# Moving eleven zero fills from GpSimd's queue to SyncE's and ScalarE's queues in a decode backward kernel

## The chip, the cores and the metric

The kernel runs on one core of a Trainium2 chip. The metric is device time in microseconds (us), the slowest core of one launch. Most executions agree within 0.3%. "Before" is the kernel without the change and "after" the kernel with it.

The engines are TensorE (PE in the profile), VectorE (DVE), ScalarE (ACT), GpSimd (POOL) and SyncE (SP). In the profile sixteen DMA engines move the data, and SyncE, ScalarE and GpSimd issue the transfers.

## The reference, cut to what matters

```python
# D 448, 16 query heads, 8 KV heads, Dh 256, caches of Sk = 32768 rows, window W = 4096, F 1792
def _fwd_reference(...):
    h  = x + attention(layernorm(x), k_cache[:, :, Sk - W:], v_cache[:, :, Sk - W:]) @ wo
    h2 = h + ((layernorm(h) @ w_gate) * (layernorm(h) @ w_up)) @ w_down
    return h2
# outputs: h2, and the gradients of h2 (against grad_out) with respect to
#          x, k_cache, v_cache, wq, wo, w_gate, w_up, w_down      -> out_0 .. out_8
```

Only the last 4,096 of 32,768 cache rows are attended to. So seven eighths of the two cache gradients (out_2 and out_3, 134 MB each) are zeros that have to be written. These zero fills are most of the kernel's bytes.

## The kernel before: the parts that matter

One large on-chip tile, the "arena", holds everything. Its first 8,192 columns (`zeros`) are the source of a 2 MB fill: 128 rows of 16 KB. The FFN later needs the second half of these columns for weights, so 13 fills of the middle read the first half twice ("half fills"). A memset gives the second half back to the fills after the FFN.

```python
HALF0, HALF1 = 42, 55
LD = nc.sync; ZQ = nc.gpsimd

def send_fills(n0, n1, halves=False):
    for reg in fills[n0:n1]:
        if halves: ZQ.dma_start(out=reg..., in_=zeros[:, 0:ZW // 2]...)   # first half, twice   (cut)
        else:      ZQ.dma_start(out=reg, in_=zeros)

send_fills(0, HALF0)                 # 42 full fills
send_fills(HALF0, HALF1, True)       # 13 half fills
...
# attention, head by head; K and V of the later heads are loaded into buffers that earlier heads free
after = {0: [("K", 3), ("V", 3)], 1: [("K", 4), ("V", 4), ("K", 5)], 2: [("V", 5)], 3: [("V", 6), ("K", 6)], 4: [("K", 7)], 5: [("V", 7)]}
for g in range(G):
    p_f = p_next
    if g + 1 < G: p_next = scores(g + 1)      # needs K of head g + 1
    moments(g, p_f)
    for kind, n in after.get(g, []): load_kv(...)          # on SyncE   (cut)
    if g == G - 2: load_wo(0)
load_wo(1)
load_block(0); load_block(1)                  # FFN weights: w_gate and w_down on SyncE, w_up on ScalarE
for n in range(3):                            # three blocks of the FFN
    ...                                       # reductions over the weights, last: dhn
    if n + 2 < 3: load_block(n + 2)
    if n == 1:
        nc.vector.memset(ar(ZW // 2, ZW // 2), 0.0)        # gives the fills their second half back
        send_fills(HALF1, len(fills))                      # 48 full fills
...
# backward of attention: 4 MB of cache gradients per head and the weight gradients, all stored by SyncE
for o, g, n0, n1, f in late_jobs:             # last 18 MB of zeros, issued by SyncE
    ...
```

## Time and profile before

| what | before | where it is read |
|---|---|---|
| time, median (lowest to highest) | 801.93 us (801.87 to 802.2) | three runs |
| span of the profiled execution | 800.5 us | first line of the page |
| bytes moved | 334.84 MB | page, part 2 |
| PE busy | 57% | page, part 1 |
| DMA engines busy | 9 tenths or more in 39 of 40 slices | page, part 2 |

These are lines of parts 2 and 3 of the page of before. Part 2 cuts the span into 40 slices of 20 us: the digit is the DMA engines' mean busy share in tenths, below it the rate. Part 3 gives packets, MB and share of time by queue: q0 is GpSimd's, q1 SyncE's, q10 ScalarE's.

```profile
DMA  9999999999999999999999999999999999999994
GB/s 350 431 430 429 428 430 430 427 428 428 431 426 422 428 417 409 420 422 428 433 423 425 424 430 428 429 426 426 424 427 423 426 420 425 423 424 427 423 440 192
q0 software_dynamic: 16496, 216.01, 63.8%
q1 hardware_dynamic: 11382, 116.68, 34.7%
q10 hardware_dynamic: 1440, 1.61, 0.6%
```

The DMA engines never rest before the last slice. So the kernel is bound by its transfers, and a change that moves no bytes away can only win in the last slice, unless packets take less time (a busy engine can also be a slow one, as skew_end_hi16k below shows). Here is that slice in steps of 2 us, from the windows view of before. After the five engines' busy times come the granted TensorE clock, the share of the 16 DMA engines that is busy, and GB/s.

```profile
786.00:788.00 2.00, 0.00 (x0) 0.00 (x0) 0.00 (x0) 0.00 (x0) 0.00 (x0) 0.50 0.79 336
788.00:790.00 2.00, 0.00 (x0) 0.00 (x0) 0.00 (x0) 0.00 (x0) 0.00 (x0) 0.50 0.54 229
790.00:792.00 2.00, 0.00 (x0) 0.00 (x0) 0.00 (x0) 0.00 (x0) 0.00 (x0) 0.50 0.27 115
...
794.00:796.00 2.00, 0.00 (x0) 0.00 (x0) 0.00 (x0) 0.00 (x0) 0.00 (x0) 0.50 0.12 49
...
798.00:800.00 2.00, 0.00 (x0) 0.00 (x0) 0.00 (x0) 0.00 (x0) 0.00 (x0) 0.50 0.02 8
```

No compute engine works any more. A share of 0.06 is one DMA engine of sixteen. The engines run dry one after the other from 786 us on, and the last one works alone to 799 us.

The records do not name the DMA engine of a packet. But packets of one engine follow each other almost without a gap (from 780 us on in before, 90% of the steps from one to the next are under 0.04 us), so they can be put into sixteen chains. Which chain is which engine stays unknown; where the chains end is clear. In before the last three end at 791.4, 795.3 and 799.0 us, and all sixteen at 790.1 us on the mean. The quantities "last end", "mean end" and "idle" below come from these chains, of one profiled execution each. The spans of nine executions of before in one batch ran from 799.9 to 801.0 us, so a difference under about 1 us between two last ends says little.

Two lines of the waits of before (engine, line, what it waited for: us in total, times, longest), six of its timeline (start, length, what; in brackets the idle time before it and what ended that; no bracket, no wait) and one of its windows will be needed again. In the timeline, 155.46 is where PE begins with the K cache of head 4:

```profile
PE ao_ps L376 <- DMA arena<-in_A_wo_dram: 10.7, 1, 10.7
PE tr_ps L252 <- DMA arena<-in_A_k_cache_dram: 8.4, 3, 3.9
```

```profile
155.46 1.07 PE L252 MATMUL tr_ps<-ident_bf,arena 128*128 128x128 bf16 x16
347.66 0.67 POOL L130 DMA_DIRECT2D out_dram<-arena  x1 [4.86 <-DMA out_dram<-arena]
366.85 0.17 DVE L406 COPY gu_f<-gu_ps 128x10 f32<-128x10 f32 x1 [12.66 <-PE gu_ps L405]
372.55 1.76 DVE L428 MEMSET arena<- 128x2048 uint32 x1 [0.41 <-DVE hh_f L409]
374.61 2.65 POOL L132 DMA_DIRECT2D out_dram<-arena  x5 [26.28 <-DVE arena L428]
484.57 56.83 SPq L648 DMA_DIRECT2D out_dram<-arena  x6
```

```profile
340.00:385.00 45.00, 14.10 (x104) 8.65 (x102) 24.39 (x54) 3.81 (x9) 4.52 (x8) 0.50 1.02 426
```

GpSimd issued its last half fill at 347.66 us, waited 26.28 us for the memset, and went on at 374.61. SyncE began to store gradients at 484.57 us.

### The profile page before, as it was taken

The numbers are of one execution on the slowest core, as the hardware profiler recorded it, in microseconds if no ns is written. First come the engines' busy times: TensorE is split into PE (matmuls) and PEld (weight loads), VectorE is DVE, ScalarE is ACT, GpSimd is POOL, SyncE is SP. The second block draws the span as 40 slices with busy tenths as digits, with TensorE's granted clock in tenths as the row PEclk, the third lists the DMA queues.
The fourth block names the chain that finished last, engine by engine and source line by source line (L and its number), as shares of the span: only waits on it lengthen the run. The fifth ranks groups of instructions, "written<-read, shape, count | busy, mean of one in ns | idle before, by whom it ended". The sixth has DMA issues, their size and how long they took to land.

```text
span 800.5 us, 8486 instructions
## 1 busy us (share of the span) xinstructions
PE 459.3 (57%) x3182; PEld 245.9 (31%) x3182; DVE 370.2 (46%) x1176; ACT 196.3 (25%) x309; POOL 62.0 (8%) x112
## 2 busy tenths in 40 slices
PE   0459999999999994623239295845262064520000
PEld 0334554545545552312129143322021022200000
DVE  2115363472552652255770975766681187660000
ACT  0143313224133100000002054643241045340000
POOL 4000000010100110101100010000000000000000
PEclk9978999999999997555559699776557567655555
DMA  9999999999999999999999999999999999999994
GB/s 350 431 430 429 428 430 430 427 428 428 431 426 422 428 417 409 420 422 428 433 423 425 424 430 428 429 426 426 424 427 423 426 420 425 423 424 427 423 440 192
DMA packets 29359, 334.84 MB, mean 418 GB/s; under 512 B 2819, under 2 KB 5894, under 8 KB 7814
## 3 DMA queue, kind: packets, MB, share of 16 engines
q0 software_dynamic: 16496, 216.01, 63.8%
q1 hardware_dynamic: 11382, 116.68, 34.7%
q10 hardware_dynamic: 1440, 1.61, 0.6%
q8 instruction: 25, 0.41, 0.2%
q14 instruction: 16, 0.13, 0.0%
HBM read 53.69 MB, written 280.59 MB: 418 GB/s over the span
## 4 chain that ended last, share of the span: by engine, by line
PE 35%; DMA 33%; DVE 15%; ACT 4%; issue 2%; another core or an unknown queue 0%; SPq 0%; ACTq 0%; DVEq 0%
DMA out_dram<-arena 19%; PE M_ps L311 11%; PE ok_ps L315 6%; PE rows_ps L255 6%; PE tr_ps L252 4%; DMA dh_bc<-in_grad_out_dram 4%; DMA arena<-in_A_k_cache_dram 4%; ACT arena L269 2%; DMA arena<-in_A_wo_dram 2%; DVE arena L645 2%; DVE arena L454 2%; DVE arena L646 2%; DMA arena<-in_B_w_up_dram 2%; PE dqb_ps L497 2%; DMA arena<-in_B_w_gate_dram 2%; DVE arena L509 2%
## 5 line engine op out<-in xcount | busy, mean ns | idle before, releaser
L307 DVE TENSOR_SCALAR arena<-arena,p_f 128x256 bf16<-128x256 bf16 x512 | 109.8, 280 | 67.0 <-PE M_ps L311 67.0
L311 PE MATMUL M_ps<-arena 128*128 128x512 bf16 x512 | 122.9, 381 | 0.0
L255 PE MATMUL rows_ps<-arena,vpad 128*16 128x512 bf16 x256 | 85.9, 431 | 22.2 <-DVE arena L608 16.9
L252 PE MATMUL tr_ps<-ident_bf,arena 128*128 128x128 bf16 x1024 | 87.9, 236 | 15.0 <-DMA arena<-in_A_k_cache_dram 8.4
L132 POOL DMA_DIRECT2D out_dram<-arena x90 | 48.8, 544 | 560.7 <-DMA out_dram<-arena 522.7
L252 PEld LDWEIGHTS <-arena 128*128 128x128 bf16 x1024 | 65.9, 105 | 65.0 <-issue 55.4
L638 PE MATMUL d_ps<-arena,rT 32*128 32x512 bf16 x256 | 43.6, 511 | 69.6 <-DVE arena L646 50.2
L269 ACT COPY arena<-tr_ps 128x1024 bf16<-128x1024 bf16 x64 | 61.7, 1015 | 87.9 <-PE tr_ps L252 87.9
L311 PEld LDWEIGHTS <-arena 128*128 128x128 bf16 x512 | 46.2, 99 | 50.8 <-issue 6.5
L315 PE MATMUL ok_ps<-arena 128*16 128x256 bf16 x512 | 57.5, 273 | 0.9 <-DVE arena L296 0.9
L606 ACT COPY arena<-tr_ps 128x1024 bf16<-128x1024 bf16 x32 | 32.5, 1016 | 96.1 <-PE tr_ps L252 39.3
L642 ACT CAST arena<-d_ps 128x512 bf16<-128x512 f32 x64 | 37.6, 588 | 71.5 <-PE d_ps L638 71.5
L645 DVE CAST arena<-d_ps 128x512 bf16<-128x512 f32 x64 | 43.9, 686 | 14.9 <-PE d_ps L638 14.6
L315 PEld LDWEIGHTS <-arena 128*16 128x16 bf16 x512 | 45.4, 90 | 13.9 <-issue 3.4
L646 DVE CAST arena<-d_ps 128x512 bf16<-128x512 f32 x64 | 43.5, 680 | 8.3 <-DMA out_dram<-arena 8.3
L638 PEld LDWEIGHTS <-rT 32*128 32x128 bf16 x256 | 11.2, 95 | 95.4 <-issue 52.1
L643 ACT CAST arena<-d_ps 128x512 bf16<-128x512 f32 x64 | 38.0, 594 | 9.1 <-DMA out_dram<-arena 9.1
L255 PEld LDWEIGHTS <-vpad 128*16 128x16 bf16 x256 | 18.9, 91 | 57.1 <-issue 49.3
L318 ACT COPY arena<-M_ps 128x512 f32<-128x512 f32 x16 | 8.6, 589 | 75.0 <-PE M_ps L311 75.0
L509 DVE CUSTOM_DVE_ANT_0 arena<-arena 128x4096 bf16<-128x4096 bf16 x3 | 13.1, 4422 | 23.1 <-ACT arena L502 23.1
L608 DVE COPY arena<-tr_ps 128x1024 bf16<-128x1024 bf16 x32 | 21.7, 680 | 4.1 <-PE tr_ps L252 4.0
L631 DVE TENSOR_SCALAR arena<-R_sb,tl_f 128x512 bf16<-128x512 bf16 x64 | 17.8, 347 | 2.1 <-ACT R_sb L628 1.9
(198 smaller groups left out, 358.1 us busy)
## 6 DMA issues: line engine op xcount, KB each, us to landing
out_dram<-arena POOLq DMA_DIRECT2D x103, 2048.0 KB, 53.5
out_dram<-arena SPq DMA_DIRECT2D x18, 2048.0 KB, 32.7
arena<-in_A_v_cache_dram SPq DMA_DIRECT2D x10, 2048.0 KB, 49.6
arena<-in_A_k_cache_dram SPq DMA_DIRECT2D x8, 2048.0 KB, 29.7
out_dram<-arena SPq DMA_DIRECT2D x4, 4096.0 KB, 57.2
arena<-in_A_wq_dram SPq DMA_DIRECT2D x2, 3072.0 KB, 20.5
arena<-in_A_wo_dram SPq DMA_DIRECT2D x2, 1792.0 KB, 16.2
out_dram<-arena SPq DMA_DIRECT2D x2, 1792.0 KB, 33.2
```

The source lines that it names most:

```text
L132: ZQ.dma_start(out=reg, in_=zeros)
L252: nc.tensor.transpose(tr_ps[:, dh, i, :], X_sb[:, 4 * q + i, dh * 128:(dh + 1) * 128], ident_bf[:])
L255: nc.tensor.matmul(rows_ps[:], lhsT=pad[:, dh, 16 * q:16 * q + 16], rhs=XT[:, dh].rearrange("p t k -> p (t k)"), start=(q == 0 and dh == 0 ...
L269: sT_ps = dots(kv_at(K_off[g]), KT_slot, vpad[g % 2], rows1, ps_c, "cols", lambda q, XT, ps: nc.scalar.copy(out=XT, in_=ps))
L307: nc.vector.tensor_scalar(out=pK[:, i, hh, :], in0=K_sb[:, t, :], scalar1=p_f[:, 8 * i + c, hh:hh + 1], scalar2=None, op0=ALU.mult)
L311: nc.tensor.matmul(M_ps[:, vh, :], lhsT=V_sb[:, t, vh * 128:(vh + 1) * 128], rhs=pK[:, i, :, :].rearrange("p h d -> p (h d)"), start=(t == ...
L315: nc.tensor.matmul(ok_ps[:, k, :], lhsT=ppad[g % 2][:, 8 * (t % 4) + t // 4, :], rhs=X_sb[:, t, :], start=(g == 0 and k == 0 and t == 0), ...
L638: nc.tensor.matmul(d_ps[:, qi].rearrange("p w d -> p (w d)"), lhsT=rT[32 * q:32 * (q + 1), :], rhs=RB_[32 * q:32 * (q + 1), l, :], start=T ...
L642: nc.scalar.copy(out=stV[:, t:t + 2, :], in_=d_ps[:, :, 0, :])
L643: nc.scalar.copy(out=stK[:, t:t + 2, :], in_=d_ps[:, :, 1, :])
L645: nc.vector.tensor_copy(out=stV[:, t:t + 2, :], in_=d_ps[:, :, 0, :])
L646: nc.vector.tensor_copy(out=stK[:, t:t + 2, :], in_=d_ps[:, :, 1, :])
```

## The change

Its intent: take work off GpSimd's queue. Of the fills, 92 stay there instead of 103. Six go on SyncE's queue behind K and V loads of the middle heads, two half fills on ScalarE's queue behind its last FFN load, three on SyncE's behind the last FFN load. The FFN loads are reordered: w_down first, the 64-row pieces ahead of the 384-row pieces, block 1 tied behind the second load of wo.

```diff
-HALF0, HALF1 = 42, 55
+HALF0, HALF1 = 36, 48
+SYNC = 11
 ...
+    own = fills[len(fills) - SYNC:]
+    fills = fills[:len(fills) - SYNC]
 ...
+    def fills_behind(eng, ins, n, halves=False):
+        with behind(ins):
+            for _ in range(n):
+                fill(eng, own.pop(), halves)
 ...
             for kind, n in after.get(g, []):
                 if kind == "K":
-                    load_kv(K_off[n], A_k_cache, n)
+                    ins = load_kv(K_off[n], A_k_cache, n)
 ...
+            if g in (2, 3, 4):
+                fills_behind(LD, ins, 2)
 ...
     def load_block(n):
+        last = [None, None]
+        LD.dma_start(out=wd, ...)                       # moved up from the end
         for eng, i, wt in ((LD, 0, B_w_gate), (nc.scalar, 1, B_w_up)):
-            eng.dma_start(out=wgu[:, 0:3, i, :], ...)
             eng.dma_start(out=wgu[0:DQ, 3, i, :], ...)
+            last[i] = eng.dma_start(out=wgu[:, 0:3, i, :], ...)
-        LD.dma_start(out=wd, ...)
+        return last
     load_block(0)
-    load_block(1)
+    with behind(wo_ins):
+        load_block(1)
 ...
-            if n + 2 < len(BLOCKS):
-                load_block(n + 2)
+            if n == 0:
+                last = load_block(2)
+                fills_behind(nc.scalar, last[1], 2, True)
             if n == 1:
                 nc.vector.memset(ar(ZW // 2, ZW // 2), 0.0)
                 send_fills(HALF1, len(fills))
+                fills_behind(LD, last[0], 3)
```

(The dots mark cuts.)

## The prediction

> **What bounds the kernel now.** Bytes: 334.84 MB in an 800.5 us span. In the windows view (20 us stretches) the mean share of the 16 DMA engines is 0.99 to 1.03 from 20 to 780 us. The chain of waits runs through PE (busy 57%), but the zero fills keep transfers going meanwhile. The only unfilled time is the start (0.92 in the first 20 us) and the end: in 2 us windows the share is about 1.0 until 786 us, then 0.79, 0.54, 0.27, 0.10, 0.12, 0.06, 0.02. One engine runs alone to 799 us, while an even share-out would end near 790. About 9 us (1.1%) is the most that reordering these bytes can win, unless packets also stall less.
>
> **What the change does.** Bytes and compute stay the same. GpSimd issues 92 fills, not 103; SyncE gets 6 behind the loads of heads 4 to 7 and 3 after the last FFN load, ScalarE 2. The Trainium skill ("DMA: Bandwidth & Descriptors", section "Issuing engines are not separate DMA queues") says the issuers share the 16 engines and interleave; the trace agrees: from 40 to 120 us GpSimd's queue moved 213 GB/s and SyncE's 214, together the full rate.
>
> 1. K of head 4 now queues behind two fills. Before, K3, V6, K4 landed at 124.1, 134.0, 144.0 us, 9.9 us apart. The build order puts two fills between K3 and V6, so K4 should land near 163.5. PE wants it at 155.5 and waits about 8 us. Later heads keep their 31.3 us cadence.
> 2. FFN: block 1's w_up load moves ahead of block 0's on ScalarE's queue, but waits there for all full-size fills (about 313 us). Block 0 is later by 5 to 10 us; block 1 and the memset that reopens the fills (before at 372.5 us) stay within 5 us.
> 3. Cover: GpSimd issued its last half fill at 347.7 us and resumed at 374.6; the fastest engine finished that batch at 376.0, the slowest at 385.0. Now 56 fills precede the memset, not 55: 4.9 us more cover. The delays should not empty the slow engine.
> 4. Fewer fills on GpSimd's queue. In a stretch of its fills alone (375 to 414 us) the last engine's lag behind the median landing grew from 6.50 to 6.96 us over 8 fills, 0.06 us each; in SyncE's tail (746 to 799 us) it fell from 9.6 to 9.35. Estimate: 11 x 0.06 = 0.6 us less lag.
>
> **On the critical path:** only point 4 and changed packet stalls. The end is set by the slowest DMA engine's total work. Compute may slip 5 to 10 us; SyncE's backlog of stores at 727 us (some 70 us long) absorbs that.
>
> **Predicted: 801.0 us, 8 in 10 between 797.0 and 804.0.** Chances: faster by over 2% 0.01, within 2% 0.97, slower by over 2% 0.02.
>
> **Right, if:** DMA stays at 1.0 up to about 786 us and the last 14 us still tail off; PE's wait for the K cache grows by about 8 us; the main stores are issued a few us later while the span hardly moves; GpSimd's queue falls from 63.8% to about 57%.
>
> **Wrong, if:** the DMA share near 340 to 385 us falls well under 1 (fills ran out before the memset); the tail after 786 us shrinks by several us (GpSimd's queue slows that engine by more than I estimate); or late stores run out of cover before the last zero fills.

## The result

After: 801.76 us (median of 4 runs, 801.49 to 801.88). Before, in the same rounds: 801.97 us (4 runs, 801.87 to 802.2). The ratio is 0.9997 with a 95% interval of 0.9979 to 1.0014: the same. The profiled spans are 800.0 and 800.5 us, with granted clocks of 0.769 and 0.764.

The lines of the page of after that answer to those of before:

```profile
DMA  9999999999999999999999999999999999999994
GB/s 351 429 432 429 427 430 428 430 431 429 427 428 427 424 424 412 418 423 423 424 428 414 427 429 430 428 428 426 423 428 421 427 421 423 425 421 426 427 437 205
q0 software_dynamic: 14784, 192.94, 57.0%
q1 hardware_dynamic: 12678, 135.55, 40.3%
q10 hardware_dynamic: 1984, 5.80, 1.8%
```

GpSimd's queue lost 23.07 MB (216.01 less 192.94), which are eleven fills of 2.097 MB. The DMA row is the same to the digit. The windows view of the end of after:

```profile
786.00:788.00 2.00, 0.00 (x0) 0.00 (x0) 0.00 (x0) 0.00 (x0) 0.00 (x0) 0.50 0.94 401
788.00:790.00 2.00, 0.00 (x0) 0.00 (x0) 0.00 (x0) 0.00 (x0) 0.00 (x0) 0.50 0.52 221
790.00:792.00 2.00, 0.00 (x0) 0.00 (x0) 0.00 (x0) 0.00 (x0) 0.00 (x0) 0.50 0.19 82
...
794.00:796.00 2.00, 0.00 (x0) 0.00 (x0) 0.00 (x0) 0.00 (x0) 0.00 (x0) 0.50 0.06 25
...
798.00:800.00 2.00, 0.00 (x0) 0.00 (x0) 0.00 (x0) 0.00 (x0) 0.00 (x0) 0.50 0.02 8
```

The tail is there as before. The last three chains end at 792.0, 794.1 and 798.7 us, the mean is 790.1 or 790.2 by how the packets are put into chains (before 790.1). Next the waits of after, its timeline, and its window from 340 to 385 us, where the prediction had named a fall of the DMA share as a sign against it:

```profile
PE tr_ps L267 <- DMA arena<-in_A_k_cache_dram: 26.7, 4, 18.0
PE ao_ps L396 <- DMA arena<-in_A_wo_dram: 6.0, 1, 6.0
```

```profile
173.70 1.89 PE L267 MATMUL tr_ps<-ident_bf,arena 128*128 128x128 bf16 x16 [17.97 <-DMA arena<-in_A_k_cache_dram]
337.27 0.67 POOL L133 DMA_DIRECT2D out_dram<-arena  x1 [8.51 <-DMA out_dram<-arena]
382.76 0.17 DVE L426 COPY gu_f<-gu_ps 128x10 f32<-128x10 f32 x1 [6.59 <-PE gu_ps L425]
383.31 1.76 DVE L449 MEMSET arena<- 128x2048 uint32 x1 [0.38 <-DVE gu_f L426]
385.37 0.55 POOL L135 DMA_DIRECT2D out_dram<-arena  x1 [47.43 <-DMA out_dram<-arena]
494.50 56.99 SPq L670 DMA_DIRECT2D out_dram<-arena  x6
```

```profile
340.00:385.00 45.00, 17.02 (x137) 11.03 (x136) 19.84 (x48) 3.10 (x9) 0.00 (x0) 0.55 1.02 423
```

So compute moved a good deal although the time did not. PE now waits 17.97 us at one place for the K cache. The memset runs at 383.31 us instead of 372.55, 10.8 us later. SyncE's stores start 9.9 us later (494.50 against 484.57). None of it reaches the end.

GpSimd's last half fill now goes out 10.4 us earlier, and it resumes 10.8 us later. (The profile puts the end of this wait down to a transfer. But GpSimd went on 0.30 us after the end of the memset, 383.31 + 1.76 us, and in before it was 0.30 us too.) ScalarE's two half fills, issued at 365.9 us, cover the difference, but for the fast engines only just: some of them are idle around 386 us, 3.7 us summed over all sixteen. The DMA share from 340 to 385 us stays at 1.02.

### The profile page after: what moved, and what is told of

Same layout as the page of the kernel before. It is cut to its first block, busy times and chain, and to the rows that moved or that the text cites. A ratio compares the mean times of both kernels' runs of the same rounds, so it can differ in the third digit from the quotient of the medians.

```text
span 800.0 us, 8481 instructions
## 1 busy us (share of the span) xinstructions
PE 459.9 (57%) x3182; PEld 246.7 (31%) x3182; DVE 370.2 (46%) x1176; ACT 196.3 (25%) x309; POOL 55.8 (7%) x101
## 3 DMA queue, kind: packets, MB, share of 16 engines
q0 software_dynamic: 14784, 192.94, 57.0%
## 4 chain that ended last, share of the span: by engine, by line
DMA 41%; another core or an unknown queue 21%; DVE 14%; PE 9%; issue 2%; POOL 2%; ACT 2%; SPq 0%; DVEq 0%; ACTq 0%; POOLq 0%
DMA out_dram<-arena 36%; DMA arena<-in_B_w_gate_dram 6%; DVE arena L667 2%; DVE arena L476 2%; DVE arena L668 2%; PE dqb_ps L519 2%; PE rows_ps L270 2%; DVE arena L531 1%; POOL out_dram L135 1%; DVE arena L556 1%; PE tr_ps L267 1%; PE d_ps L660 1%; DVE arena L443 1%; PE dqb_ps L522 1%
## 5 line engine op out<-in xcount | busy, mean ns | idle before, releaser
L267 PE MATMUL tr_ps<-ident_bf,arena 128*128 128x128 bf16 x1024 | 88.6, 237 | 31.9 <-DMA arena<-in_A_k_cache_dram 26.7
L135 POOL DMA_DIRECT2D out_dram<-arena x80 | 43.3, 542 | 547.1 <-DMA out_dram<-arena 546.8
```

Source lines behind the costliest of these rows:

```text
L135: eng.dma_start(out=reg, in_=zeros)
L267: nc.tensor.transpose(tr_ps[:, dh, i, :], X_sb[:, 4 * q + i, dh * 128:(dh + 1) * 128], ident_bf[:])
```

## The experiments

Theory T: the end is the total work of the slowest DMA engine, plus the time in which that engine had nothing queued. Delays of compute are free as long as transfers stay queued. The rivals are:

- M: PE's longer wait costs real time.
- G: fills on GpSimd's queue slow one DMA engine, and so set the tail. This is point 4 of the prediction.
- Some runs have rivals of their own, named in their expectations.

All twelve kernels gave correct results. Before was run beside each batch: its medians were 802.24, 802.03, 802.07 and 802.3 us (9 runs each).

| run | what it is | us, median | ratio to before, 95% | last end | mean end |
|---|---|---|---|---|---|
| before | | 801.97 | | 799.0 | 790.1 |
| after | | 801.76 | 0.9997 [0.9979, 1.0014] | 798.7 | 790.2 |
| k4_first | SyncE's six fills one head later | 801.23 | 0.9989 [0.9976, 1.0003] | 798.1 | 790.1 |
| k4_short | that, without ScalarE's half fills | 801.43 | 0.9991 [0.9979, 1.0004] | 798.4 | 790.9 |
| ffn_only | FFN half of the change alone | 801.70 | 0.9995 [0.9981, 1.0009] | 798.3 | 790.4 |
| attn_only | attention half alone | 812.04 | 1.0124 [1.0110, 1.0138] | 808.4 | 805.2 |
| no_act_cover | after, without ScalarE's half fills | 811.62 | 1.0119 [1.0105, 1.0132] | 809.2 | 806.2 |
| gpsimd_tail | last 18 MB issued by GpSimd | 806.48 | 1.0051 [1.0038, 1.0063] | 798.3 | 791.4 |
| probe_tail | markers at the very end | 803.01 (one look) | | | |
| skew_hi | lopsided fill in mid-program | 861.67 | 1.0747 [1.0729, 1.0765] | | |
| skew_lo | the same, other engines meant | 862.21 | 1.0745 [1.0728, 1.0761] | | |
| skew_end_lo | lopsided fill at the end, first eight engines | 806.32 | 1.0052 [1.0040, 1.0065] | 803.0 | 790.2 |
| skew_end_hi | the same, second eight meant | 810.12 | 1.0104 [1.0091, 1.0118] | 806.8 | 799.4 |
| skew_end_hi16k | the same with other rows | 810.86 | 1.0109 [1.0090, 1.0128] | 807.3 | 798.2 |

The batches ran on three chips (5, 1 and 9).

### k4_first: PE's long wait taken away

```diff
-            if g in (2, 3, 4):
+            if g in (3, 4, 5):
                 fills_behind(LD, ins, 2)
```

> The six middle fills go behind the loads of heads 6 and 7 instead of before V6, K5 and K4, so head 4's K load no longer queues behind two fills. All theories expect PE's wait for the K cache to fall from 26.7 us to about 8 and the memset before the reopened fills to come some 10 us earlier than in the changed kernel (383.3 us). Theory T (the end is the slowest DMA engine's total work, and compute only has to keep it fed): 801.7 us, within 0.5 us. Rival M (the changed kernel has a real gain of several us that the 18 us wait of PE gives back): 2 to 10 us faster, 792 to 800 us.

The wait fell from 26.7 to 9.0 us in total, its longest piece from 18.0 to 4.3. The line is from the waits of k4_first:

```profile
PE tr_ps L267 <- DMA arena<-in_A_k_cache_dram: 9.0, 3, 4.3
```

The memset came at 374.89 us, 8.4 us earlier than in after, and no DMA engine was idle after 300 us. Yet the time is 801.23 us. Rival M falls: giving back 17.7 us of PE's waiting moved the last end by 0.6 us, and the interval still holds 1.

### no_act_cover: the fills that bridge the gap taken away

```diff
-SYNC = 11
+SYNC = 9
 ...
-                fills_behind(nc.scalar, last[1], 2, True)
```

(The two fills return to GpSimd's queue behind the memset.)

> The two half fills on ScalarE's queue go back to GpSimd, behind the memset; the 18 us wait stays. The fast DMA engines then have only small loads from about 374 us until the memset at about 383 us: a dip of the DMA share to under 0.6 there, 5 to 9 us lost on most engines. Theory T: the slowest engine still has work until about 385 us, so the end moves by at most +2 us (801.5 to 803.8), and the tail after 786 us gets steeper (share still near 1 at 790 us). Rival M (mean DMA throughput is the bound, so lost mean time is lost): +5 to +9 us, 807 to 811 us.

It cost 1.2%. From the page of no_act_cover:

```profile
DMA  9999999999999999996699999999999999999997
GB/s 351 430 431 430 429 426 432 429 429 431 426 424 426 423 425 410 418 424 270 266 426 401 423 428 430 429 425 426 424 427 423 428 420 426 422 423 420 429 437 323
```

The two sixes are the slices from 365 to 405 us (a slice is 20.3 us here): the DMA engines ran dry. The slowest engine was idle for 8.76 us, all sixteen for 14.35 us on the mean. The last end moved by 10.5 us (798.7 to 809.2), the mean end by 16.0 (790.2 to 806.2). This fits T in kind: the last end moved by 1.7 us more than the slowest engine's idle time, and the mean end by 1.7 us more than the mean idle time. So each follows its own idle time, and the 1.7 us are common to both; where they come from is open. My number was wrong, because I did not see what the build would do with the memset. Here it stands behind the weight reductions of block 1 (gu_f at 383.99 us, memset at 389.76). In after it follows gu_f after 0.55 us.

All seven kernels of this family show the same split. With ScalarE's half fills the memset comes 0.5 to 0.6 us after gu_f (after, k4_first, ffn_only); without them 5.7 to 5.8 us (before, no_act_cover, k4_short, attn_only). The program text has the memset in the same place in all of them. What in the build decides it was not tried.

### attn_only and ffn_only: one half of the change each

```diff
 attn_only, against after:                      ffn_only, against after:
-HALF0, HALF1 = 36, 48                          -HALF0, HALF1 = 36, 48
-SYNC = 11                                      -SYNC = 11
+HALF0, HALF1 = 36, 49                          +HALF0, HALF1 = 42, 54
+SYNC = 6                                       +SYNC = 5
 (load_block and its order as in before,        -            if g in (2, 3, 4):
  no fills behind FFN loads)                    -                fills_behind(LD, ins, 2)
```

> Only the first part of the change: six fills behind the loads of the middle heads, the FFN loads and their order as before, 55 fills before the memset. All expect PE's wait for head 4's K near 27 us in total and the memset 15 to 18 us later than before (388 to 391 us). Theory T: the slowest engine runs out near 385 us and idles 4 to 7 us, so 806 to 809 us; the FFN part of the change is then what pays for the delay. Rival M: the mean idle, 10 to 14 us, is added: 812 to 816 us. If fills on SyncE's queue are worth something by themselves, it would show as less than the slow engine's idle time.

> Only the FFN half of the change (two half fills on ScalarE, three fills on SyncE behind the last FFN load, the new order of the FFN loads); no fill stands before the K and V loads of the middle heads. T (the end is the slowest DMA engine's total work plus any time it was empty): PE's longest wait for the K cache is about 4 us as before, the stretch before the memset stays covered, no empty DMA time, ends last near 798.5, time 801.7 +-0.5 us, no difference from before that 5 rounds can see. Rival (moving fills off GpSimd's queue is itself worth something in this half): 801 or less, or a last engine that ends over 1 us earlier.

The attention half alone costs 1.2%. From the page of attn_only:

```profile
DMA  9999999999999999998499999999999999999997
GB/s 352 429 430 429 430 429 426 429 432 426 425 430 423 426 423 419 419 426 367 180 425 396 426 432 430 426 427 430 421 426 422 428 423 428 421 423 421 430 437 314
```

PE waits 28.2 us for the K cache, the memset slips to 393.37 us, the slowest engine idles for 8.12 us and the mean engine for 13.94. The last end is 9.4 us later than in before and the mean end 15.1, again both a little more (1.3 and 1.2 us) than the idle time. The FFN half alone changes nothing: its longest K wait is 5.1 us, the memset comes at 366.17 us, no engine is idle, and the last end is 798.3 us. So the two halves do not add up: the second half pays for the delay that the first one makes. Together they are worth nothing, and each of them has a different price alone.

### k4_short: no early fills, no bridge

```diff
 against k4_first:
-HALF0, HALF1 = 36, 48
-SYNC = 11
+HALF0, HALF1 = 36, 49
+SYNC = 9
 ...
-                fills_behind(nc.scalar, last[1], 2, True)
```

> As k4_first (no wait on head 4's K), but without ScalarE's two half fills and with one more on GpSimd: 55 fills before the memset, as in the original kernel, and the build places the memset behind the weight reductions, so fills reopen near 381 us. The fast DMA engines should run out near 376 us, the slowest near 385. This is the case that no_act_cover missed: fast engines idle some 5 us, the slowest not at all. Theory T (the end follows the idle time of the slowest engine): within 1 us of k4_first's 801.2. Rival M (mean DMA time lost is lost): +4 to +5 us, 805 to 806.

Only four gaps, some 3 us in sum, appeared around 382 us, far less idle time than I had meant to make. The 376 and 385 us of the expectation come from the same misreading as in the prediction: the last of the 55 fills landed from 381.4 us on, and GpSimd resumed at 381.3. The time is 801.43 us. That is consistent with T, but the lever was too small to tell much.

### probe_tail: which engines are the slow ones

The last 2 MB fill of after was cut short. What was cut off was written after it, by small SyncE transfers whose row counts let only 15, 14, 8, 7 and 1 engines take part.

```diff
 ...                                            (cut: the loop before leaves out the last 2 MB fill)
+        m = 128 * (ZW - 32)
+        LD.dma_start(out=flat[0:m].rearrange("(p f) -> p f", p=128), in_=ar(ZW, ZW - 32))
+        a = m
+        for k in (15, 14, 8, 7):
+            LD.dma_start(out=flat[a:a + 32 * k].rearrange("(p f) -> p f", p=k), in_=ar(ZW, 32)[0:k])
+            a += 32 * k
+        LD.dma_start(out=flat[a:128 * ZW].rearrange("(p f) -> p f", p=1), in_=ar(ZW, 128 * ZW - a)[0:1])
```

> The changed kernel with the last 2 MB fill cut short by 16 KB and four tiny writes over 15, 14, 8 and 7 engines behind it, as thermometers: the landing times of each show when the engines it uses had finished everything before it. Theory T expects one engine alone to be about 4 to 5 us behind the second and 9 us behind the median, as in the changed kernel (last engines at 798.7, 794.1, 792.0 us), the same one whatever queue the fills came from; the skill's page names engines 7 and 15 as usually slow, so landing 798.7 should be missing from the write over 15 engines if it is the last engine. If it is present in the write over 7 engines the slow one is among the first seven. Time about 802 us.

The Trainium skill ("DMA: Bandwidth & Descriptors", section "Why a DMA increments its semaphore by 16 and not by 1") says that a transfer issued by SyncE on k engines uses the k lowest-numbered ones. The landings of this run, us, one per engine:

```
16 engines: 788.18 788.19 788.33 788.48 788.50 788.81 789.13 789.89 790.23 790.42 790.73 790.74 793.40 795.13 796.49 799.28
 8 engines: 790.84 790.94 791.24 791.33 793.94 795.66 797.08 799.84
 7 engines: 791.11 791.41 791.52 794.11 795.83 797.28 800.02
```

The four late landings stay when eight engines take part, and also when only seven do. So the four slow engines are among the first seven, if the skill's rule holds; the run agrees with it, since each smaller set of landings continues the larger one. In the write over eight, the first eight engines end at 790.8 to 799.8 us, 793.9 on the mean. In the write over sixteen, which comes before it, the same eight end at 790.2 to 799.3, 793.3 on the mean, and the second eight at 788.2 to 789.9, 788.7 on the mean. The same page ("Latency and other measured facts") says that engines 7 and 15 are usually the slower ones. This run does not agree: neither is among its four slowest.

### gpsimd_tail: does GpSimd's queue slow an engine?

The 18 MB of zeros that SyncE issues last (nine fills of 2.097 MB) were given to GpSimd, as nine more fills on its queue.

```diff
-        for o, g, n0, n1, f in late_jobs:
-            reg = zero_rows(o, g, n0, n1, f)
-            for i in range(reg.shape[0]):
-                LD.dma_start(out=reg[i], in_=ar(2 * ZW - f, f))
 (these regions are in `fills` instead, and go out through send_fills; cut: a late memset of
  their source falls away, and SyncE's eleven fills write other regions)
```

> The late zero fills (18 MB, nine fills' worth) move from SyncE's queue at the end to GpSimd's, the opposite of the change. Rival G (each fill on GpSimd's queue costs the last engine 0.06 us, the estimate of the prediction): +0.5 us, 802.3 us; if the cost per fill were larger the end would move with it (0.3 us each would be +2.7). Theory T: nothing but the slowest engine's own work matters: within 0.5 us of 801.7, as long as GpSimd's window of eight fills keeps that engine fed to the end; the share after 786 us falls off as before.

The last end was 798.3 us against 798.7 in after. By point 4 of the prediction it should have been 9 x 0.06 = 0.5 us later. G is not seen, but 0.5 us is within the scatter of single executions; what this run rules out is a large cost, such as the 0.3 us a fill of the expectation. But the kernel still got slower, by 0.5%, for another reason. These are one line of the end of gpsimd_tail (its last source line, sequencer instructions: durations in ns as least, median and most; first and last start in us) and two of its windows view:

```profile
L699 POOLq DRAIN  x3: 45/93/62558, 740.3 to 803.4; - x3
```

```profile
796.00:800.00 4.00, 0.00 (x0) 0.00 (x0) 0.00 (x0) 0.00 (x0) 0.00 (x0) 0.50 0.03 12
800.00:804.00 4.00, 0.00 (x0) 0.00 (x0) 0.00 (x0) 0.00 (x0) 0.00 (x0) 0.50 0.00 0
```

and the same line of after:

```profile
L705 POOLq DRAIN  x3: 45/102/59307, 687.9 to 799.8; - x3
```

After its last issue GpSimd drains. In gpsimd_tail this takes 62.56 us from 740.3, so to 802.9 us, 4.6 us after the last packet of its queue (798.3). In after it takes 59.31 us from 687.9, to 747.2, 4.3 us after its last packet (743.0), where it costs nothing. So with the last transfers on GpSimd's queue the program ended 5.3 us after its last packet (803.6 less 798.3), and in after 1.3 us (800.0 less 798.7).

### skew_hi and skew_lo: a lopsided fill, first attempt

One 2 MB fill of GpSimd's was to load eight engines with 16 packets each, instead of sixteen with 8 each. T expects the last end to move by 8 packets of 0.61 us = 4.9 us, up or down by which eight it is.

```diff
 skew_hi, against k4_first (skew_lo: without the first write, rows of 8192):
+        ZQ.dma_start(out=flat[0:8 * 512].rearrange("(p f) -> p f", p=8), in_=zeros[::16, 0:512])
+        ZQ.dma_start(out=flat[8 * 512:].rearrange("(p k f) -> p k f", p=8, k=16), in_=zeros[::16, 0:8160].unsqueeze(1).to_broadcast([8, 16, 8160]))
```

> k4_first with one 2 MB fill of GpSimd's queue sent through 8 engines only, after a tiny 8-engine write that should move GpSimd's starting point on by 8 (the skill's DMA page, how many engines). The thermometers put the four slow ends in engines 0 to 6 and engines 8 to 15 at 788.2 to 790.2 us, 0 to 7 at 790.8 to 799.3. Theory T: the lower half is freed of 128 KB (4.9 us) each and the upper half gets as much more, so the end comes 4 to 4.9 us earlier than in k4_first: 796.3 to 797.2 us, and the tail is shorter. If the end is set by anything else (queue of issue, compute, mean throughput): no gain, or a few us lost to the lopsided transfer. If the starting point does not move it behaves as skew_lo.

> The same lopsided fill without the tiny write before it, so that it should fall on engines 0 to 7. Theory T: the slow engine gets 128 KB more than its share, 4.9 us, and the end comes that much later than in k4_first: 805.5 to 806.5 us, one engine running alone for longer. Mean throughput is the same as in skew_hi, so a rival that bounds the kernel by the mean expects both alike.

("The skill's DMA page" is "DMA: Bandwidth & Descriptors", section "Why a DMA increments its semaphore by 16 and not by 1": a GpSimd transfer on fewer than sixteen engines takes consecutive ones from a cursor that goes round. No run here shows that cursor.)

Both took about 60 us more. They say nothing of T, because the fill stopped the whole program. Two lines of the waits of skew_hi:

```profile
DVE arena L446 <- DMA out_dram<-arena: 166.9, 1, 166.9
PE bc_ps L450 <- DVE arena L446: 171.8, 4, 168.4
```

VectorE waited 166.9 us for a store to leave the arena before it wrote a part of the arena that the fill does not read. In the built program the lopsided fill also waits for other arena loads, unlike its neighbours. The likely reason is that a source with a row step counts as a read of the whole arena; that was not tested by itself. Its packets were slow too, 1,689 ns on the mean against 623 for the other 16 KB packets of GpSimd's queue in this run.

### skew_end_lo and skew_end_hi: the lopsided fill at the end

Now it is the last transfer that GpSimd issues, so nothing is left to wait for it. It replaces SyncE's last 2 MB fill.

```diff
 skew_end_lo, against k4_first:
-    late_jobs = [..., (out_3, G - 1, 6, 7, ZW)]
+    late_jobs = [...]
+        ZQ.dma_start(out=flat.rearrange("(p k f) -> p k f", p=8, k=16), in_=ar(0, ZW)[0:32:4].unsqueeze(1).to_broadcast([8, 16, ZW]))
 skew_end_hi:
+        ZQ.dma_start(out=flat[0:8 * 512].rearrange("(p f) -> p f", p=8), in_=ar(0, 512)[0:32:4])
+        ZQ.dma_start(out=flat[8 * 512:].rearrange("(p k f) -> p k f", p=8, k=16), in_=ar(0, ZW - 32)[64:96:4].unsqueeze(1).to_broadcast([8, 16, ZW - 32]))
```

> The same without the small write, so that the 2 MB go to the first eight engines, to which the slow ones belong. T: the last engine gets 4.9 us more work: last landing near 803.5, time about 806 us. R: no change, 801 to 802. If both skewed kernels move the same way, the share of the engines is not what separates them and T is not supported.

> The lopsided fill again, now as the last transfer that GpSimd issues, from 8 partitions that lie apart, so that no later write of the program can wait for it. It replaces SyncE's last 2 MB fill (16 engines, 8 packets each) by 2 MB on 8 engines only (16 packets each), meant for the second eight by a small 8-row write before it. T: in the last stretch the first eight engines do 8 packets x 0.61 us = 4.9 us less and the second eight 4.9 us more. The probe had the first eight ending at 790.8 to 799.8 and the second at 788.2 to 790.2, so now 786 to 794.5 and 793 to 795: the last landing near 795, time about 797.5 us (k4_first 801.2 less some 3.7), which would beat both kernels. Rival R (the end is set by the fabric or by the order of the fills, not by each engine's own sum): no change, 801 to 802. If the second eight are not those meant: near +4.9 us.

skew_end_lo did what T expects. Its windows view at the end:

```profile
784.00:788.00 4.00, 0.00 (x0) 0.00 (x0) 0.00 (x0) 0.00 (x0) 0.00 (x0) 0.50 0.49 213
788.00:792.00 4.00, 0.00 (x0) 0.00 (x0) 0.00 (x0) 0.00 (x0) 0.00 (x0) 0.50 0.46 197
792.00:796.00 4.00, 0.00 (x0) 0.00 (x0) 0.00 (x0) 0.00 (x0) 0.00 (x0) 0.50 0.46 197
796.00:800.00 4.00, 0.00 (x0) 0.00 (x0) 0.00 (x0) 0.00 (x0) 0.00 (x0) 0.50 0.17 74
800.00:804.00 4.00, 0.00 (x0) 0.00 (x0) 0.00 (x0) 0.00 (x0) 0.00 (x0) 0.50 0.04 16
```

From 784 to 796 us about half the engines work. The chains end in two groups: eight from 779.7 to 785.1 us (mean 782.7) and eight from 793.7 to 803.0 (mean 797.7). The means lie 15.0 us apart. In the probe (on another chip) the two groups lay 4.6 us apart (793.3 less 788.7); with 2 x 4.9 us of added difference that makes 14.4, near the 15.0 measured. The last end moved from 798.1 in k4_first to 803.0, the expected 4.9 us, while the mean end stayed (790.1 and 790.2). Rival R, by which no engine's own sum matters, falls.

skew_end_hi should have won 3.7 us and lost 8.1 against before (810.12 against 802.07). Its 16,320 B packets took 1,105 ns on the mean. Beside them, from 735 to 745 us, the median 32 KB packet of SyncE's queue took 2,511 ns; in skew_end_lo it was 1,219. The rate fell to 277 GB/s from 740 to 760 us.

### skew_end_hi16k: are the odd rows the cause?

```diff
 against skew_end_hi:
-        ZQ.dma_start(out=flat[0:8 * 512].rearrange("(p f) -> p f", p=8), in_=ar(0, 512)[0:32:4])
-        ZQ.dma_start(out=flat[8 * 512:]... k=16), in_=ar(0, ZW - 32)[64:96:4]...to_broadcast([8, 16, ZW - 32]))
+        ZQ.dma_start(out=flat[0:8 * ZW].rearrange("(p f) -> p f", p=8), in_=ar(0, ZW)[0:32:4])
+        ZQ.dma_start(out=flat[8 * ZW:]... k=15), in_=ar(0, ZW)[64:96:4]...to_broadcast([8, 15, ZW]))
```

> skew_end_hi with rows of 16,384 B at 16,384 B steps, where that run had rows of 16,320 B: the last 2 MB as one row for each of the first eight engines and fifteen rows for each of the second eight, in place of eight and eight. In skew_end_hi the 16,320 B packets took 1,105 ns on the mean and the 32,768 B packets of SyncE's queue beside them up to 2,511 ns, against 617 and 1,221 in skew_end_lo. Theory S (those rows were slow for their length and start, not for the engines they went to) with T: packets 611 to 630 ns, no slow stretch, the first eight engines 7 x 0.61 = 4.3 us less than in k4_first (last 798.1, so 793.8), the second eight 4.3 us more (790.2 in the probe, so 794.5): last landing near 795, time about 797.4 us, ratio near 0.994, faster than both kernels. Rival (the second eight engines, or the source rows 64 to 92, make it slow): packets near 1,100 ns again and 808 to 811 us. Rival R (no engine's own sum matters): 801 to 802.

No. With rows of 16,384 B the time is 810.86 us. The packets from 745 to 755 us took 1,140 ns on the mean, and the windows view shows the slow stretch again, with a DMA share of 1.01 but only 269 GB/s:

```profile
735.00:755.00 20.00, 0.00 (x0) 0.00 (x0) 0.00 (x0) 0.00 (x0) 0.00 (x0) 0.50 1.01 269
```

Theory S is refuted: length and start of the rows are not the cause. What the two slow runs share, and skew_end_lo does not have, is the small write before and the source rows 64 to 92.

I think that the small write did not turn the fill to the second eight engines. Two things point that way. First, the eight early chains of this run end 8.8 to 10.2 us after those of skew_end_lo, rank by rank, so they look like the same eight engines. Second, in the chains the slow 32 KB packets mostly stand on other engines than the slow fill packets, as if each engine of the fill shared a source with an engine that does not take part in it. The skill fits this reading. The section that was named for the probe states an exception: some copies issued by GpSimd get all sixteen engines, with the row count divided by sixteen and rounded up for each. By it, if these copies are among them, eight rows give one each to the first eight engines, every time. And "The descriptor swizzle" on the same page gives, for a transfer of 128 rows, rows 64 to 92 to the ports of the second eight engines, so the first eight would have read through ports of the others. No run tried rows 64 to 92 without the small write. So this is argued and not shown, and whether work can be taken from the slow engines stays open. No version beat both kernels by more than the noise: k4_first has the lowest median (801.23), and its interval against before holds 1.

## Why the prediction was right, point by point

The time was right: 801.0 predicted, 801.76 measured, inside the range and the same as before. In part this was luck, as points 2 and 3 show: the delays were larger than predicted, and cover that the prediction had not counted made up for them. The main argument held: the DMA engines are full, so the end is set by the slowest DMA engine's total work, and slips of compute vanish. k4_first, ffn_only and after differ by up to 17 us in when the memset runs and by 14 us in PE's longest wait, and lie within 0.6 us in time and in last end. skew_end_lo moved one engine's work alone and the end followed it. attn_only and no_act_cover show the limit: when the slowest engine itself runs dry for 8 to 9 us, the end moves by 9 to 11 (the surplus of 1.3 to 1.7 us is not explained).

1. **K of head 4.** The mechanism was right and the size was wrong: 8 us predicted, 17.97 measured. I took "K3, V6, K4 landed at 124.1, 134.0, 144.0 us". The built program issues V6, K5, K4, so the third of these is K5. K4 landed at 153.9, only 1.5 us before PE wanted it (155.46). Two fills at 9.9 us each put it to 173.7. In after V6 landed at 154.1, K5 at 163.9 and K4 at 173.65, and PE went on at 173.70.
2. **FFN.** That block 1 and the memset stay within 5 us was wrong: the memset came 10.8 us later. (The first gu_f, of block 0, came 15.3 us later, 346.80 instead of 331.49, where 5 to 10 were predicted; that of block 1 came 16.1 us later.) The end of the attention moved by the K4 wait too; the second load of wo was issued at 320.68 us instead of 300.93, 19.8 us later. Nine of these were made up: PE's wait for wo fell from 10.7 to 6.0 us, and the memset followed gu_f after 0.55 us where it had been 5.70. The prediction had neither of these savings, and had not carried the K wait, let alone its full size, through wo to the memset.
3. **Cover.** "The delays should not empty the slow engine" was right, but the sum behind it was not. The 376.0 and 385.0 us are the landings of the last half fill but one; the right ones, 380.9 and 389.9, give 4.9 us more cover than was counted. With one more fill of 4.9 us the fastest engine should last to about 385.8 us and the slowest to about 394.8 (an estimate from these landings). GpSimd resumed at 385.37: fast engines were idle near 386 us for 3.7 us in sum, and the slowest was not. Without the nine microseconds of point 2, which the prediction did not contain, GpSimd would have resumed near 394 by the same estimate, with next to nothing left for the slowest engine. That part was luck. The two fills on ScalarE's queue are needed in any case; no_act_cover shows what they are worth: 10 us.
4. **GpSimd's queue.** The estimate of 0.06 us lag for each fill is not seen. The last end was 0.3 us earlier in after, which could be it or not. But gpsimd_tail put nine fills back and ended 0.4 us earlier, where the estimate says 0.5 later. Differences as small as these cannot be told from scatter, so an effect of this size is neither shown nor excluded. Over all the runs whose slowest DMA engine never ran dry and whose fills were not lopsided, the last end lies between 798.1 and 799.0 us, whatever queue the fills were on. What made the lag grow in the stretch that I had read is open.

The signs named in the prediction came out as follows. DMA at about 1.0 up to 786 us with a tail after it: yes. Wait for the K cache up by 8 us: no, by 18.3 in total (26.7 less 8.4). Main stores later while the span hardly moves: yes, by 9.9 us, a little more than "a few". GpSimd's queue at about 57%: yes, 57.0%. The signs against it did not show: the DMA share from 340 to 385 us is 1.02 as before, and the tail did not shrink. The skill's statement that all issuers share the same 16 engines ("Issuing engines are not separate DMA queues") was borne out: 23 MB changed queues, and no slice before the last changed its rate by more than 11 GB/s.

Not explained is why four engines end later than the rest. Nothing tried here touched it. The record narrows it: from 745 us on all 32 KB packets of before and after took 1,211 to 1,232 ns, whichever chain they are in. So in the tail no engine is slower per packet; the late ones are behind. In before the last engine was 9.6 us behind the median landing at 737 us already, and 9.35 us at 790 us, but in GpSimd's fills up to 180 us it was never more than 3 us behind: the lag was built up in between.

## What to carry to other kernels

When all DMA engines are busy from start to end, ask what the slowest engine has to do in total and whether it ever runs dry; which queue issues a transfer, and how long compute waits, made no difference here as long as it did not (except for GpSimd's drain at the very end). Before moving filler transfers in front of loads, read the order in which the built program issues those loads, since here each 2 MB in front delayed all that followed by 9.9 us while two queues shared the rate. Test the halves of a change alone: here one half cost 1.2%, and the other half hid it.

## What the Trainium skill lacked or had wrong

- "DMA: Bandwidth & Descriptors", section "Latency and other measured facts": engines 7 and 15 are called usually slower. In probe_tail the four slowest engines are among the first seven, 3 to 9 us behind the others at the end of an 800 us kernel; the second eight, 15 among them, end within 1.7 us of each other and are the fastest.
- No page that I read says how long GpSimd's end drain outlasts its last transfer. It ended 4.3 us after the last packet of GpSimd's queue in after (in k4_first and ffn_only 4.3 and 4.5 us) and 4.6 us after it in gpsimd_tail, where it lengthened the kernel by 0.5%. In before it was 0.8 us (drain to 746.3, last packet 745.5); why is open.
- "DMA: Bandwidth & Descriptors" does not say what a fill costs whose eight engines read rows of other engines' ports, if that is what happened: fill packets of 1,140 ns (745 to 755 us) instead of 617, SyncE's 32 KB packets beside them up to 2,550 ns instead of 1,220, and 269 GB/s (735 to 755 us of skew_end_hi16k) where skew_end_lo moved 423 (740 to 760 us).
